# DeltaNet attention and an MLP in one kernel: VectorE's constants and GpSimd's row selector moved to the beginning, W1's first half asked for later

## The chip, the cores and the metric

The kernel runs on one core of a Trainium2 chip. The metric is the time of one launch in device microseconds (us), the median of several runs. The core has five engines that run their own instruction streams and meet at semaphores: TensorE (PE; its weight loads are listed as PEld), VectorE (DVE), ScalarE (ACT), GpSimd (POOL) and SyncE (SP, which here only issues DMA). Sixteen DMA engines move data between HBM and the on-chip memory SBUF; matmuls write PSUM, eight banks of accumulators.

## The reference

```python
B, H, S, D = 4, 8, 768, 48
k_n = k / (np.linalg.norm(k, axis=-1, keepdims=True) + 1e-06)
state = np.zeros((B, H, D, D))
for t in range(S):
    kt, vt, bt = k_n[:, :, t], v[:, :, t], beta[:, :, t, None]
    y[:, :, t] = np.einsum('bhd,bhde->bhe', q[:, :, t], state)
    v_old = np.einsum('bhde,bhd->bhe', state, kt)
    state = state + bt[:, :, :, None] * np.einsum('bhd,bhe->bhde', kt, vt - v_old)
x = y.transpose(0, 2, 1, 3).reshape(B * S, H * D)      # 3072 x 384
h = x @ w_in                                            # 384 x 2048
g = 0.5 * h * (1.0 + np.tanh(c * (h + 0.044715 * h * h * h)))   # c = sqrt(2/pi)
return g @ w_out                                        # 3072 x 384
```

A recurrent delta rule over 768 steps for 32 heads, then an MLP on its output.

## The kernel before

The 768 steps are cut into 12 chunks of 64 (c = 0 to 11). A chunk has two units, u = 2c and 2c + 1, of 8 heads for two batches each. Per chunk the recurrence becomes matrix work: the keys are normed and turned, their products (a lower triangle) are inverted, the state is carried from chunk to chunk, and the chunk's 256 rows go through the MLP, 16 `up` and 8 `down` groups of matmuls.

The steps carry names, and the name's number is the unit or the chunk. Those that follow come up below, roughly in the order of the data:

- `k2.01`, `q1.11`, `v0.00`, `k0x0.01`: loads of a chunk's k, q, v in four pieces (line 472). Chunk 0's k comes in two halves, `k0x1` and `k0x0`. Three buffers per input, so chunk c + 3 overwrites chunk c.
- `sq`, `sum`, `pow`, `eps`, `inv` (lines 495 to 503): the norms of the keys, on ScalarE, VectorE and, for `eps` sometimes, GpSimd. `0a` and `0b` are the halves of chunk 0.
- `kn` or `knc` (lines 531, 524): keys times inverse norm; `qb`, `qbc`, `vb`, `vbc`: casts of q and v to bf16.
- `Tk`, `Tq`, `T` (line 540): transposes on TensorE, copied back by `kTk`, `kTq`, `kT` (line 343); `GD`, `GQ`, `G` (line 564): products of keys with keys and queries, read by `dn` (copy) and `wq` (masked copy, line 571).
- `F`, `lp`, `x0`, `L`, `xm`, `xa`, `xb` (lines 633 to 669): the inverses of the 8x8 blocks, `xm1` to `xa6` step by step on VectorE. `F` uses the constant `sel`, `L` the constant `rows`.
- `xe`, `xec`, `KZ`, `kz`, `GM`, `lw`, `X10`, `X11`, `A4`, `rt4`, `B4`, `bde4`, and so on (lines 599 to 723): the inverse of the whole triangle.
- `V`, `R`, `U`, `Un`, `S`, `Sn`, `O`, `On`, `X`, `xT` (lines 756 to 811): state and output of a chunk; `up`, `gelu`, `down`, `Z` (lines 824 to 840): the MLP.
- `betaT`, `betaN`, `betaH`, `betaL`, `betaS`, `betaC` (lines 437 to 460): beta is turned and spread once.
- Constants, made once: `sel` (line 391), `unit` (394), `rowz` and `rows1` (381, 382: `rows` is zeroed, then GpSimd sets its ones), `two` (380), `wz` (355), `muq` (369), `low1` (396), `first0` (400, a column of a leaf buffer), `triwq` and `trilw` (411 on GpSimd, 343 elsewhere: patterns in the buffers of `wq` and `lw`), `ladj` (418, patterns in a right-hand side), `pad` (403) and `bdz` (421, zeroes).

Nothing is scheduled at run time. The text `ORDER` lists every step once with its engine (`:d` VectorE, `:g` GpSimd, `:a` ScalarE, `:s` SP, none for TensorE) and its PSUM bank (`@4`). `Flow.order` (line 151) fills one queue per engine from it, and `Flow.emit` (line 190) puts semaphore waits where an operand comes from another engine. An engine runs its queue strictly in the order of the text, so a step that waits holds everything behind it on its engine. Of two GpSimd steps for different halves of the partitions, the later waits for the earlier.

The weights are loaded by GpSimd's DMA queue, in two halves each. W1's halves (`w1.0`, `w1.1`) are declared as readers of chunk 1's k buffer, so that they come after its load:

```python
A(("pool",), f"w1.{i}", lambda e, P, f0=f0: e.dma_start(W1[:, :, f0:f0 + FF // 2], w1v[:, :, f0:f0 + FF // 2]),
  reads=["kraw10", "kraw11"], writes=[f"W1{i}"], dma=f"w1{i}")
```

Chunk 4's k goes to the same buffer, and so its four loads wait for both halves of W1. They stand in SP's queue behind all earlier loads.

Of the kernel before, what the change touches and what calls it, by code (L numbers as in the profile page):

```python
# [21 lines left out]
muq1:g ladj4.0:a k2.01:s betaN011:d pow.1:a betaN110:d eps.1:g pad3:d k2.11:s inv.1:d triwq1:d betaN010:d low1:d kn.2:d v0.10:s kn.3:d qb.1:a Tk.2@7
v0.01:s qb.0:g Tk.3@5 kTk.2:d q2.01:s rows1:g Tq.1@4 sq.0a:a betaN111:d kTk.1:d q2.10:s kTq.1:d kTk.3:a sum.0a:d q2.00:s GD.3@4 betaH1:d pow.0a:a
Tq.0@7 sq.2:a eps.0a:d rpad0:g v1.00:s inv.0a:d GD.2@2 betaN000:d GD.1@0 dn.3:a kn.0:g betaL1:d q1.01:s betaH0:d betaS1@6 dn.2:a sum.2:d low2:g
q1.00:s dn.1:a Tk.0@4 first0:d F.1@2 kTq.0:d pow.2:a q1.10:s eps.2:g kTk.0:d trilw2:g q1.11:s GQ.1@0 lp.1:d GD.0@4 betaL0:d x0.1:d L.1@7 q3.01:s
dn.0:a two:d inv.2:d GQ.0@2 wz:d knc.2:g xm1.1:d qbc.2:a F.0@4 k3.00:s wq.0:d xa1.1:d q3.10:s betaS0@5 xm2.1:d xa2.1:d betaS3@2 w1.0:g lp.0:d k3.11:s
betaC0:a xm3.1:d ladj5.1:d L.0@3 triwq2:a ladj4.1:d T.5@4 v0.00:s x0.0:d wqa.1:a xm1.0:d first1:g xa1.0:d kT.5:a qb.3:g xa3.1:d xm2.0:d v0.11:s
xa2.0:d trilw3:g Tq.3@0 xm4.1:d xm3.0:d betaC1:a xa3.0:d qb.2:g xa4.1:d xm5.1:d xm4.0:d T.4@6 xa4.0:d xa5.1:d betaS2@1 xm5.0:d xm6.1:d kT.4:a xa6.1:d
xa5.0:d Tq.2@4 kTq.3:d xb.1:g xm6.0:d triwq5:g xa6.0:d betaC2:a xb.0:d G.5@6 w1.1:g kTq.2:a xe.1:d G.4@0 dn.4:a v2.11:s xe.0:d KZ.1@4 kz.1:a wq.4:d
mwp1:g dn.5:a GM.1@4 xec.1:d KZ.0@0 ladj5.0:a F.2@3 wqa.5:a betaC3:a lw.1:d kz.0:a lp.2:d bdz1:d L.2@3 k3.01:s GM.0@4 x0.2:d X10.1:g KZ.2@6 lw.0:d  # L30
KZ.3@0 kz.3:a X11.1:g kz.2:a xm1.2:d GM.3@0 xa1.2:d rpad1:g A4.1@2 X11.0:g lw.3:d X10.0:g rt4.1:d k3.10:s xm2.2:d A4.0@1 X11.3:g xa2.2:d v1.01:s
B4.1@2 xm3.2:d xa3.2:d rt4.0:d q3.11:s GQ.2@6 GM.2@4 vb.0:a xm4.2:d vb.1:g wq.2:d k4.11:s B4.0@1 bde40.1:a triwq3:g lw.2:d V.0@6 X10.3:g k4.01:s
bde41.1:a bde40.0:a k4.00:s wqb.1:g xa4.2:d A4.3@2 xm5.2:d bde41.0:a A5.1@0 k4.10:s rt4.3:d GQ.3@4 R.0:a rt5.1:d A5.0@1 X11.2:g B4.3@2 v1.10:s rt5.0:d
B5.1@0 bde40.3:a xa5.2:d q3.00:s B5.0@7 X10.2:g xm6.2:d fill115@1 xa6.2:d be50.1:d be50.0:a v1.11:s wq.3:d xb.2:g be51.1:a A4.2@3 sq.3:a w2.0:g
be51.0:d v2.01:s xe.4:d U.0@0 bde41.3:d KZ.4@4 Un.0:a w2.1:g rt4.2:d kz.4:a O.0@6 sum.3:d A5.3@4 On.0:a S.0@2 rt5.3:d GM.4@0 sq.4:a xe.5:d X.0@6
B4.2@7 lw.4:d Sn.0:a fill85@4 KZ.5@4 xT.0:a sum.4:d X11.4:g bde40.2:a up4.0@2 kz.5:d pow.3:g up0.0@0 bde41.2:a up1.0 X10.4:d tabG:a up2.0 up12.0@6
qbc.3:d up3.0 A5.2@4 up13.0 rt5.2:d gelu0.0:a up5.0 up6.0 GM.5@4 eps.3:d inv.3:d knc.3:d up7.0 up14.0 A4.4@0 lw.5:d up15.0 turn.7:s B5.2@1 gelu3.0:a
rt4.4:d up8.0@4 X11.5:g up9.0 gelu1.0:a B5.3@0 vbc.1:g down00.0@6 be50.3:d up10.0 be51.3:a X10.5:d pow.4:g be50.2:a up11.0 V.1@2 gelu2.0:a T.6@0
v2.00:s A4.5@7 kT.6:d v2.10:s be51.2:a K.1 down01.0 R.1:a rt4.5:d q5.00:s G.6@4 k5.10:s B4.5@7 dn.6:a B4.4@2 xi4.5:d U.1@0 bde40.4:a down02.0 k5.00:s
wq.6:d bdc40.5:g Un.1:a down03.0 k5.01:s bde41.4:d bdc41.5:g eps.4:g A5.5@1 k5.11:s Z0.0:d wqb.5:g S.1@4 Q.1@2 q4.11:s Sn.1:d G.7@6 O.1 vbc.2:g  # L40
q4.01:s A5.4@0 rt5.5:d On.1:a down10.0@5 inv.4:d q4.10:s dn.7:d kn.9:g down11.0 rt5.4:d q4.00:s wq.7:d F.3@1 q5.01:s B5.4@4 lp.3:d V.2@2 sq.5:a x0.3:d
v3.10:s L.3@1 B5.5@0 xm1.3:d X.1@6 be50.4:a v3.01:s be50.5:a xa1.3:d K.2 be51.5:a xm2.3:d down12.0 be51.4:a xa2.3:d q5.11:s xT.1:d R.2:a down13.0
xm3.3:d q5.10:s xa3.3:d xm4.3:d qbc.4:g up0.1@2 xa4.3:d Z1.0:a up12.1@6 xm5.3:d xa5.3:d up1.1 kn.8:g xm6.3:d sum.5:d turn.9:s U.2@4 up13.1 Un.2:a
up14.1 xa6.3:d pow.5:g xb.3:d up15.1 xec.3:d Q.2@0 gelu3.1:a S.2@4 turn.8:s O.2 up2.1 Sn.2:d On.2:a up3.1 up8.1@6 gelu0.1:a qb.11:d up9.1 KZ.6@0
eps.5:d KZ.7@4 inv.5:d kz.6:a up10.1 kn.11:d up11.1 kz.7:a up4.1@0 kn.10:g turn.11:s qb.10:a GM.6@2 gelu2.1:a G.9@4 lw.6:d up5.1 up6.1 dn.9:a up7.1
# [858 lines left out]
```

## Time and profile before

| what | value |
|---|---|
| median of 3 runs | 254.64 us (254.40 to 255.61) |
| span of the profiled execution (no other time is given for it) | 254.7 us |
| PE busy over the span | 226.0 us (89%) |
| DVE busy over the span | 185.8 us (73%) |
| ACT busy over the span | 157.4 us (62%) |
| POOL busy over the span | 130.1 us (51%) |
| mean granted TensorE clock | 0.966 |

The profile is one execution. Its page has the busy time of each engine, the span in 40 slices of 6.4 us (a digit is the busy share in tenths; PEclk is the granted clock of TensorE in tenths of full speed), the DMA queues, the chain of waits that ended last, and groups of equal instructions:

```profile
PE   0259558899999998999999899999999999999994
DVE  6599989955996989898888779898494665755100
POOL 7647448347563397627358968472535525330000
PEclk9999956689999999999999999999999999999999
```

The first eight slices are the start that the change touches. Beside the page the trace can be asked for a stretch: the time line gives start and length in us, engine, line, operation, what it writes and reads, how many were merged, and in brackets the idle time of the engine ahead of it and what ended it. The waits of SP's queue are a view of their own:

```profile
SPq L472 <- DMA W<-in_moe_w_in_dram: 5.9, 1, 5.9
```

That is one wait of 5.9 us, of the k loads of chunk 4 for W1.

### The profile page before, as it was taken

The numbers are of one execution on the slowest core, as the hardware profiler recorded it, in microseconds if no ns is written. First come the engines' busy times: TensorE is split into PE (matmuls) and PEld (weight loads), VectorE is DVE, ScalarE is ACT, GpSimd is POOL, SyncE is SP. The second block draws the span as 40 slices with busy tenths as digits, with TensorE's granted clock in tenths as the row PEclk, the third lists the DMA queues.
The fourth block names the chain that finished last, engine by engine and source line by source line (L and its number), as shares of the span: only waits on it lengthen the run. The fifth ranks groups of instructions, "written<-read, shape, count | busy, mean of one in ns | idle before, by whom it ended". The sixth has DMA issues, their size and how long they took to land.

```text
span 254.7 us, 12256 instructions
## 1 busy us (share of the span) xinstructions
PE 226.0 (89%) x5500; PEld 178.3 (70%) x5502; DVE 185.8 (73%) x445; ACT 157.4 (62%) x244; POOL 130.1 (51%) x159
## 2 busy tenths in 40 slices
PE   0259558899999998999999899999999999999994
...
DVE  6599989955996989898888779898494665755100
...
POOL 7647448347563397627358968472535525330000
PEclk9999956689999999999999999999999999999999
...
GB/s 103 165 144 118 184 162 95 165 127 117 128 130 105 112 126 124 135 165 147 119 146 167 100 36 131 147 153 130 56 93 167 62 49 4 33 68 64 3 93 62
DMA packets 104532, 28.25 MB, mean 111 GB/s; under 512 B 98592, under 2 KB 103712, under 8 KB 104480
## 3 DMA queue, kind: packets, MB, share of 16 engines
q1 hardware_dynamic: 99200, 23.79, 54.0%
...
q8 instruction: 43, 0.70, 1.2%
q10 hardware_dynamic: 2400, 0.54, 1.1%
...
HBM read 20.64 MB, written 4.72 MB: 100 GB/s over the span
## 4 chain that ended last, share of the span: by engine, by line
PE 73%; DVE 15%; ACT 4%; DMA 2%; ACTq 2%; issue 2%; SPq 1%; POOL 0%
PE ps L835 24%; PE ps L824 22%; PE ps L692 5%; PE ps L620 3%; PE ps L752 3%; PE ps L773 2%; DMA vraw<-in_v_dram 2%; PE ps L697 2%; PE ps L564 2%; DVE lw L623 2%; DVE xl L658 2%; PE ps L633 2%; PE ps L759 2%; DVE ps L655 2%; PE ps L609 1%
## 5 line engine op out<-in xcount | busy, mean ns | idle before, releaser
L824 PE MATMUL ps<-xT,W 128*128 128x256 bf16 x576 | 76.8, 277 | 0.4 <-DVE xl L658 0.4
L835 PE MATMUL ps<-W,gT 128*128 128x384 bf16 x384 | 72.7, 326 | 0.0
L828 ACT ACTIVATE gT<-ps 128x1024 bf16<-128x1024 f32 x48 | 48.4, 1022 | 26.4 <-PE ps L824 25.8
L824 PEld LDWEIGHTS ps<-xT,W 128*128 128x128 bf16 x576 | 52.2, 99 | 9.3 <-DVE xl L658 0.5
L835 PEld LDWEIGHTS ps<-W,gT 128*128 128x128 bf16 x384 | 34.0, 97 | 18.2
L682 POOL TENSOR_SCALAR_AFFINE_SELECT bd<-lw 64x512 bf16<-64x512 bf16 x34 | 22.6, 667 | 37.7 <-DVE lw L623 28.6
L704 DVE TENSOR_TENSOR rl<-ps,two 128x384 bf16<-128x384 f32 (+1 forms) x48 | 22.9, 484 | 9.7 <-PE ps L692 9.5
L623 DVE CAST_PREDICATED lw<-mlw,ps 128x832 bf16<-128x832 uint16 x24 | 24.3, 1018 | 6.8 <-PE ps L620 6.5
L499 POOL TENSOR_TENSOR nrm<-nrm,half 128x16 f32<-128x16 f32 x9 | 26.6, 2956 | 2.8 <-DVE nrm L497 2.7
L343 ACT ACTIVATE bd<-ps 32x256 bf16<-32x256 f32 (+1 forms) x40 | 16.8, 428 | 8.2 <-PE ps L692 4.4
L692 PEld LDWEIGHTS ps<-lw,bd 128*128 128x128 bf16 x384 | 15.5, 98 | 4.2 <-POOL bd L682 1.2
L692 PE MATMUL ps<-lw,bd 128*128 128x32 bf16 (+1 forms) x384 | 17.2, 183 | 1.2 <-POOL bd L682 1.1
L658 DVE TENSOR_TENSOR xl<-ps,xl 128x96 bf16<-128x96 f32 (+4 forms) x72 | 16.0, 228 | 2.0
L655 DVE TENSOR_TENSOR ps<-ps,xl 128x64 f32<-128x64 f32 (+5 forms) x72 | 15.6, 221 | 2.0 <-PE ps L649 0.5
L343 ACT ACTIVATE ob<-ps 128x384 f32<-128x384 f32 x17 | 8.3, 490 | 14.0 <-PE ps L835 14.0
L722 POOL COPY bd<-xi 64x256 f32<-64x256 f32 x20 | 8.0, 401 | 16.4 <-ACT xi L343 8.5
L540 PE MATMUL ps<-ident,tok 128*128 128x128 bf16 x80 | 7.8, 246 | 8.1 <-POOL tok L531 3.8
L531 POOL TENSOR_TENSOR tok<-kraw,nrm 128x384 bf16<-128x384 f32 x9 | 8.5, 945 | 12.7 <-DVE bsb L349 5.6
L349 ACT ACTIVATE kT<-ps 128x512 bf16<-128x512 f32 x18 | 10.4, 596 | 6.4 <-PE ps L609 6.4
L343 ACT ACTIVATE dn<-ps 128x512 bf16<-128x512 f32 x18 | 10.4, 593 | 5.3 <-PE ps L564 5.3
L620 PE MATMUL ps<-kT 48*64 48x56 bf16 (+1 forms) x768 | 11.1, 196 | 2.8 <-ACT kT L349 1.4
L599 POOL TENSOR_TENSOR zt<-xb,blk 128x2048 bf16<-128x2048 bf16 x3 | 10.9, 3642 | 4.1 <-DVE xb L669 3.9
...
## 6 DMA issues: line engine op xcount, KB each, us to landing
qraw<-in_q_dram SPq DMA_DIRECT2D x48, 96.0 KB, 3.6
vraw<-in_v_dram SPq DMA_DIRECT2D x48, 96.0 KB, 3.5
kraw<-in_k_dram SPq DMA_DIRECT2D x44, 96.0 KB, 3.6
...
out_dram<-ob SPq DMA_DIRECT2D x3, 96.0 KB, 2.2
```

The costliest lines, as they stand in the source:

```text
L343: return e.activation(out, in_, ACT.Copy) if e is nc.scalar else e.tensor_copy(out, in_)
L499: if e is nc.scalar else e.tensor_tensor(nr[:, 1, hx], nr[:, 0, hx], half[:, hx], ALU.pow), reads=[nrn, "half"] + ["one"] * (c < ROOTS),
L620: ins = e.matmul(P(ps("GM"))[hf(a), o_ + c0:o_ + c1], kT[s][r, y, g, hf(a)], kT[s][r, z, g, C * a + c0:C * a + c1])
L623: A(("dve",), op("lw"), lambda e, P: e.copy_predicated(lw[m][:, :, 0:LW - LB], mlw[:, :, :].rearrange("p w t -> p (w t)")[:, 16:16 + LW - ...
L655: A(("dve",), f"xm{m}.{c}", lambda e, P, m=m, w=w, part=part: e.tensor_tensor(part(P), P(f"L.{c}")[:, off[m]:off[m] + 2 * H * w].rearrange ...
L658: A(("dve",), f"xa{m}.{c}", lambda e, P, m=m, part=part: e.tensor_tensor(xl[y][:, :, m + 1:LB], part(P), xl[y][:, :, m + 1:LB], ALU.add), ...
L682: A(("pool", "dve"), op(f"X1{a}"), lambda e, P, src=lw[m][hf(a), :, LW - C:LW], dst=bd[b_][hf(a), :, hf(a)], a=a: e.affine_select(out=dst, ...
L692: ins = e.matmul(P(name)[:, C * h + c0:C * h + c1], bd[b_][:, h, :], rhs[:, h, :])
L704: A(("dve",), op(f"rt{i}"), lambda e, P, i=i, c0=c0, c1=c1, r_=r_: e.tensor_tensor(r_[:, 0:H, c0:c1], P(ps(f"A{i}")).rearrange("p (h t) -> ...
L824: ins = e.matmul(P(ph)[:, 256 * f:256 * f + 256].rearrange("p (x t) -> p x t", x=2), W1[:, j, 128 * (i + f):128 * (i + f) + 128], x_[:, :, ...
L828: A(("act",), f"gelu{i // 4}.{c}", lambda e, P, i=i, ph=ph: e.activation(g_[:, i:i + 4, :], P(ph).rearrange("p (f t) -> p f t", f=4), ACT. ...
L835: ins = e.matmul(P(po)[:, 0:DM], g_[:, f, 128 * b:128 * b + 128], W2[:, f, :], start=(f == 0), stop=(f == FC - 1))
```

## The change

Only the text `ORDER` differs; every step is the same and stays on its engine. On VectorE, `two`, `wz`, `ladj5.1` and `ladj4.1` go ahead of `sel`; `first0` behind `unit`; `bdz1` behind `muq`; `triwq1`, `pad3` and `low1` ahead of `sum.0b`; and `inv.1`, `kn.2`, `kn.3` ahead of three of the `betaN` copies. On GpSimd, `rowz` and `rows1` go behind `triwq0`, `triwq4` behind `qb.0`, and `w1.0` behind `qb.3`, `trilw3` and `qb.2`, the casts of chunk 1's queries. Of the text, one line of before and the two that stand in its place:

```diff
-ident2:g bdz0:g k0x1.01:s k0x1.11:a mmlw:d identf:d blk2:g k1.00:s beta00:a blk3:g k0x0.00:a k1.10:s half:g own:g triwq4:g trilw1:a k1.11:s sel:d
+ident2:g bdz0:g k0x1.01:s k0x1.11:a mmlw:d identf:d blk2:g k1.00:s beta00:a blk3:g k0x0.00:a k1.10:s half:g own:g trilw1:a k1.11:s two:d wz:d
+ladj5.1:d ladj4.1:d sel:d q0.10:s k0x0.10:a unit:d first0:d betaT1@0 triwq0:g rowz:g rows1:g q0.01:s mmuq:d bdz1:d mln0:g tabS:a bdz2:g sq.0b:a
```

How the queues change is shown at three places, rows with their line, operation and tile; a minus is a row of before that is gone from there, a plus one that is there now. First the beginning of VectorE's queue, from the memset of the mask `mlw` to the first beta copy (`sel` is line 391, `unit` 394, `muq` 369):

```order
 L368 MEMSET mlw 128x128
 L364 TENSOR_SCALAR identf<-tmpl 32x32
+L380 TENSOR_SCALAR two<-tmpl 128x64
+L355 MEMSET wz 128x256
+L418 TENSOR_SCALAR rl_1<-tmpl 128x8x32
+L418 TENSOR_SCALAR rl_1<-tmpl 128x8x16
 L391 TENSOR_TENSOR sel<-ident,own 128x1024
 L394 TENSOR_REDUCE unit<-ident 128x8
+L400 CAST xl<-unit 128x16
 L369 MEMSET muq 128x64
+L421 MEMSET bd 128x512
 L349 TENSOR_SCALAR bsb<-ps 64x22x4
```

`two`, `wz` and both `ladj` now stand ahead of `sel`, `first0` behind `unit`, `bdz1` behind `muq`. GpSimd's queue at the same time, from the memset of `half` and the sum `own` on, which `sel` reads:

```order
 L367 MEMSET half 128x16
 L390 TENSOR_TENSOR own<-blk 128x64
-L411 COPY wq<-tmpl 128x256 x2
+L411 COPY wq<-tmpl 128x256
+L381 MEMSET rows 128x512
+L382 AFFINE_SELECT rows<-rows 128x1024
 L372 AFFINE_SELECT mlw<-mlw 64x64
 L421 MEMSET bd 128x512
 L403 MEMSET tok 128x16x8
 L374 AFFINE_SELECT mlw<-mlw 64x64
-L381 MEMSET rows 128x512
```

One of two pattern copies has left, and the row selector (line 382) has come with its memset, 10 rows earlier than before. Second place, VectorE from `sum.1` (line 497) to the first `kT` copy of chunk 1 (line 343); line 503 is `inv.1`, line 531 are `kn.2` and `kn.3`, line 349 the `betaN` copies:

```order
 L497 TENSOR_REDUCE nrm<-sq 128x16
+L503 RECIPROCAL nrm<-nrm 128x16
+L531 TENSOR_TENSOR tok<-kraw,nrm 128x8x48 x2
 L349 TENSOR_SCALAR bsb<-ps 64x2x4
 L349 TENSOR_SCALAR bsb<-ps 64x22x4
-L403 MEMSET tok 128x16x8
-L503 RECIPROCAL nrm<-nrm 128x16
-L343 COPY wq<-tmpl 128x512
 L349 TENSOR_SCALAR bsb<-ps 64x2x4
-L396 MEMSET low 128x1
-L531 TENSOR_TENSOR tok<-kraw,nrm 128x8x48 x2
 L343 COPY kT<-ps 128x512
```

The two products follow `inv.1` at once; the pad, the pattern and the memset have gone to the beginning. Third place, GpSimd from the pattern copy `trilw2` and chunk 2's key product `knc.2` (line 524) to `xb.1` (line 669):

```order
 L411 COPY lw<-tmpl 128x448
 L524 TENSOR_TENSOR tok<-kraw,nrm 128x2x8x48
-L481 DMA W<-in_moe_w_in_dram 128x3x1024
 L400 CAST xl<-unit 128x16
 L343 CAST tok<-qraw 128x8x48
 L411 COPY lw<-tmpl 128x448
 L343 CAST tok<-qraw 128x8x48
+L481 DMA W<-in_moe_w_in_dram 128x3x1024
 L669 TENSOR_TENSOR xb<-xl,bc 128x128
 L411 COPY wq<-tmpl 128x256
```

The request for W1's first half has passed four steps. The one for the second half stays where it was, behind `xb.1` and a pattern copy. VectorE in the same stretch, from `lp.0` (line 637) on, in the queue before:

```order
L637 TENSOR_TENSOR lp<-ps,bsb 128x112
L655 TENSOR_TENSOR ps<-ps,xl 128x64
L418 TENSOR_SCALAR rl_1<-tmpl 128x8x32
L418 TENSOR_SCALAR rl_1<-tmpl 128x8x16
L640 SCALAR_TENSOR_TENSOR xl<-lp,unit 128x16x7
L655 TENSOR_TENSOR ps<-ps,xl 128x96
```

and in the queue of the change:

```order
L637 TENSOR_TENSOR lp<-ps,bsb 128x112
L655 TENSOR_TENSOR ps<-ps,xl 128x64
L640 SCALAR_TENSOR_TENSOR xl<-lp,unit 128x16x7
L655 TENSOR_TENSOR ps<-ps,xl 128x96
L658 TENSOR_TENSOR xl<-ps,xl 128x16x6
```

The two `ladj` (line 418) no longer stand ahead of `x0.0` (line 640) and `xm1.0`. TensorE, ScalarE and SP keep their queues as they were.

More of the change, by code (lines that the diff above doesn't have):

```diff
@@ L22 @@
[L22 to L45, printed above, removed]
@@ new lines @@
+k2.00:s pad4:g mwp0:g betaN101:d triwq1:d pad3:d low1:d k0x0.11:a betaT0@6 sum.0b:d q0.00:s betaN100:d mln1:g pow.0b:a q0.11:s eps.0b:d pad1:g
+inv.0b:d betaN001:d sq.1:a kn.1:g q2.11:s k0x0.01:a sum.1:d k2.10:s muq0:g Tk.1@1 muq1:g ladj4.0:a k2.01:s pow.1:a eps.1:g k2.11:s inv.1:d kn.2:d
+v0.10:s kn.3:d qb.1:a Tk.2@7 v0.01:s qb.0:g triwq4:g Tk.3@5 betaN011:d betaN110:d betaN010:d kTk.2:d q2.01:s Tq.1@4 sq.0a:a betaN111:d kTk.1:d q2.10:s
+kTq.1:d kTk.3:a sum.0a:d q2.00:s GD.3@4 betaH1:d pow.0a:a Tq.0@7 sq.2:a eps.0a:d rpad0:g v1.00:s inv.0a:d GD.2@2 betaN000:d GD.1@0 dn.3:a kn.0:g
```

27 lines of the change are left out of this document (23 added, 4 removed).

## The prediction

> **What bounds the kernel now.** I read the busy times by stage first, then the chain of waits up to the first MLP matmul, and then the time lines of VectorE and GpSimd beside each other. In the two stage rows the columns behind the stage's length are busy microseconds (and instructions) of PE, PEld, DVE, ACT and POOL, then the granted TensorE clock.
>
> ```profile
> span 254.7 us, 12256 instructions
> 22.00:34.00 12.00, 6.93 (x212) 5.60 (x203) 11.53 (x39) 8.96 (x17) 5.97 (x10) 0.95 0.96 155
> 50.00:100.00 50.00, 49.09 (x1294) 38.79 (x1293) 40.18 (x98) 37.56 (x60) 29.94 (x28) 0.97 0.79 123
> ```
>
> From 50 us on TensorE is busy 49 of each 50 us, in an order that the change leaves alone: this part can start earlier or later, hardly run shorter. Before it, from 22 to 34 us, VectorE is busy 11.53 of 12 us and TensorE only 6.93. So a start of 50 us that VectorE bounds is followed by a rest that TensorE bounds. The chain of waits over the first 51 us says the same (start, length, what):
>
> ```profile
> 12.39 0.43 DVE wq L343
> 13.06 1.97 DVE tok L531
> 20.21 0.11 DVE xl L400
> 50.01 1.18 PE ps L824 x5
> ```
>
> It runs mostly over VectorE until the first `up` (line 824) at 50.01, and pieces of it are constants that nobody needs yet: `triwq1` at 12.39, `first0` at 20.21. So a microsecond taken out of this stretch should start the MLP a microsecond earlier.
>
> **Part A, 11.5 to 15.7 us.**
>
> ```profile
> 12.17 0.50 POOL L343 CAST tok<-qraw 128x384 bf16<-128x384 f32 x1
> 12.31 0.51 DVE L343 COPY wq<-tmpl 128x512 bf16<-128x512 bf16 x1
> 12.63 2.05 POOL L382 TENSOR_SCALAR_AFFINE_SELECT rows<-rows 128x1024 bf16<-128x1024 bf16 x1
> 13.06 1.96 DVE L531 TENSOR_TENSOR tok<-kraw,nrm 128x384 bf16<-128x384 f32 x1
> 14.95 0.54 DVE L531 TENSOR_TENSOR tok<-kraw,nrm 128x384 bf16<-128x384 f32 x1
> 15.72 0.42 DVE L343 COPY kT<-ps 128x512 bf16<-128x512 bf16 x1 [0.23 <-PE ps L540]
> ```
>
> `kn.2` (13.06) and `kn.3` (14.95) are the same instruction, yet the first takes 1.96 us and the second 0.54. The first ends 0.3 us after GpSimd's row selector `rows1` (12.63 + 2.05 = 14.68): it stood still for about 1.4 us beside the selector. The change takes the selector away from there, and `pad3`, `triwq1` and `low1` from in front of `kn.2`; three beta copies move behind `kn.3`. `inv.1` keeps its place, since it waits for GpSimd, and ends at 12.39, where the chain goes on with `triwq1`. Then `kn.2` runs from 12.39 to 12.9 at best. GpSimd's query cast (until 12.67) and the `triwq4` behind it may hold the two products in the same way, so `kn.2` ends at 13.2 at worst, and `kn.3` between 13.4 and 13.9 instead of 15.49. The three beta copies come next (about 0.5 together), and the first `kT` copy starts between 13.9 and 14.4 instead of 15.72. That is 1.3 to 1.8 us; I take **1.5**. What is late next is chunk 0's last k load, for which `sq.0a` waits:
>
> ```profile
> 13.85 0.52 ACT L495 ACTIVATE sq<-kraw 128x384 f32<-128x384 f32 x1 [1.19 <-DMA kraw<-in_k_dram]
> ```
>
> It is done at 14.37; its reader `sum.0a` stands on VectorE behind three `kT` copies, which would end near 15.7. The load stays hidden.
>
> **Part B, 20 to 22.3 us.** `first0`, `two` and `wz` leave.
>
> ```profile
> 20.14 0.18 DVE L400 CAST xl<-unit 128x16 bf16<-128x16 f32 x1
> 21.77 0.43 PE L564 MATMUL ps<-kT 48*64 48x64 bf16 x16
> 22.29 0.67 DVE L571 CAST_PREDICATED wq<-muq,ps 128x512 bf16<-128x512 uint16 x1
> ```
>
> `first0` holds 0.11 of the chain, so **0.1**. `two` and `wz` I put at 0: the masked copy at 22.29 reads what the matmuls leave at 22.20, and those do not wait for the two. The upper end is the 0.35 that they hold on VectorE.
>
> **Part C, 23.9 to 25.4 us.**
>
> ```profile
> 23.45 1.01 POOL L481 DMA_DIRECT2D W<-in_moe_w_in_dram  x1
> 23.79 0.22 DVE L655 TENSOR_TENSOR ps<-ps,xl 128x64 f32<-128x64 f32 x1
> 23.92 0.94 DVE L418 TENSOR_SCALAR rl<-tmpl 128x256 bf16<-128x256 bf16 x2
> 24.62 0.59 POOL L343 CAST tok<-qraw 128x384 bf16<-128x384 f32 x1
> 24.78 0.56 DVE L640 SCALAR_TENSOR_TENSOR xl<-lp,unit 128x112 bf16<-128x112 bf16 x1
> 25.38 0.27 DVE L655 TENSOR_TENSOR ps<-ps,xl 128x96 f32<-128x96 f32 x1
> 34.12 0.20 DVE L640 SCALAR_TENSOR_TENSOR xl<-lp,unit 128x112 bf16<-128x112 bf16 x1
> ```
>
> The two `ladj` copies take 0.94 us beside the issue of W1's first half on GpSimd, and `x0.0` takes 0.56 beside a GpSimd cast, against 0.20 for the same shape at 34.12. Without the copies `x0.0` starts at 24.01 and `xm1.0` at 24.3 to 24.4 instead of 25.38: 1.0 us. If a query cast, which W1 no longer holds back, lies beside `x0.0` again, 0.6 is left. I take **0.9**, since the cast would mostly be over. W1's issue now falls among the `xm` and `xa`, which take one operand from PSUM; the `xm` at 23.79, beside the issue, and at 25.38, beside other GpSimd work, show 0.22 and 0.27 for 64 and 96 elements, so it costs them nothing.
>
> **Part D, nothing.** `bdz1` (0.48 us, now at 33.7) stands ahead of `lw.0`, which waits for TensorE in any case:
>
> ```profile
> 34.79 1.02 DVE L623 CAST_PREDICATED lw<-mlw,ps 128x832 bf16<-128x832 uint16 x1 [0.46 <-PE ps L620]
> ```
>
> If TensorE were not in the way, `bdz1` could give 0.4; I put it at 0. W1's first half is needed at 50 us and asked for at about 23.5, as before: 0.
>
> **Where the moved work goes.**
>
> ```profile
> 4.62 1.38 DVE L391 TENSOR_TENSOR sel<-ident,own 128x1024 bf16<-128x1024 bf16 x1 [1.22 <-POOL own L390]
> 7.35 0.24 DVE L349 TENSOR_SCALAR bsb<-ps 64x88 f32<-64x88 f32 x1 [0.98 <-PE ps L437]
> 9.00 0.55 DVE L497 TENSOR_REDUCE nrm<-sq 128x8 f32<-128x384 f32 x1 [1.40 <-ACT sq L495]
> 10.32 0.83 POOL L531 TENSOR_TENSOR tok<-kraw,nrm 128x384 bf16<-128x384 f32 x1 [1.86 <-DVE bsb L349]
> ```
>
> VectorE idles 1.22 us before `sel` (for `two`, `wz` and the `ladj`: 1.38 at their present lengths, less if they no longer stand beside a DMA issue), 0.98 before 7.35 (for `first0` and `bdz1`: 0.66) and 1.40 before 9.00 (for `triwq1`, `pad3`, `low1`: 0.74). GpSimd idles 1.86 us before 10.32; the selector (2.05) comes in there and `triwq4` (0.4) goes out. By length all fit, and what is 0.2 over before `sel` finds 0.3 before 7.35. Cost 0.
>
> **The sum:** 1.5 + 0.1 + 0.9 = 2.5 us. Against the profiled execution (span 254.7; the page shows no time around it, and the median of the runs, 254.64, lies within 0.1) that is **252.2 us**. The lower ends give 1.3 + 0.1 + 0.6 = 2.0 (252.7), the upper ones 1.8 + 0.45 + 1.0 + 0.4 = 3.6 (251.1).
>
> **Rival 1: the stall moves with the selector.** In its new place the selector starts when `sel` ends, near 6.0, and runs to 8.0, and `first0` lies beside it. A cast of this shape has stood still beside GpSimd work:
>
> ```profile
> 18.45 0.88 POOL L531 TENSOR_TENSOR tok<-kraw,nrm 128x384 bf16<-128x384 f32 x1 [3.69 <-DVE bsb L349]
> 18.56 0.80 DVE L447 CAST bhl<-bsb 128x16 bf16<-128x16 f32 x1
> ```
>
> That is 0.80 against the 0.18 of `first0` at 20.14. All that is queued behind `first0` on VectorE (`muq`, `bdz1`, a beta copy, `triwq1`, `pad3`, `low1`: about 1.6 us) would start at 8.0, and `sum.0b` at 9.6 instead of 9.00; for it wait, over ScalarE, chunk 0's last k load, `sq.1`, `sum.1` and `inv.1`. GpSimd's query cast would have cost `kn.2` up to 0.3 of these 0.6 anyway, so I price it at 0.3 to 0.6, 0.5 taken: **252.7**. [...]
>
> **Rival 2: loads that keep their absolute time.** Behind the landings below stands the median time from issue; q0 is GpSimd's queue from 26 to 30 us.
>
> ```profile
> 29.16 0.81 POOL L481 DMA_DIRECT2D W<-in_moe_w_in_dram  x1
> q0 software_dynamic: 326, 0.67, 92.9%
> vraw<-in_v_dram SPq DMA_DIRECT2D x1, 96.0 KB, 8.8
> 38.96 0.59 ACT L343 ACTIVATE bd<-ps 64x512 bf16<-64x512 f32 x1 [2.24 <-PE ps L692]
> 38.11 3.40 SPq L472 DMA_DIRECT2D kraw<-in_k_dram  x4
> kraw<-in_k_dram SPq DMA_DIRECT2D x4, 96.0 KB, 3.4
> 43.78 1.81 POOL L483 DMA_DIRECT2D W<-in_moe_w_out_dram  x2
> 47.38 0.84 ACT L495 ACTIVATE sq<-kraw 128x768 f32<-128x768 f32 x1
> ```
>
> While W1 moves, it takes 92.9% of the DMA engines, and a load issued behind it needs 8.8 us. Its second half, behind `xb.1`, would be asked for at 26.7 instead of 29.16, so that both halves run without a gap to 35 or 38 us, and chunk 0's v may have to wait for their end. On ScalarE `vb.0`, now done at 36.7 (2.24 us before 38.96), may end at 36.5 without harm, so v may land by 36.0. At 38 the gain is down to 0.5: **254.2**.
>
> **Rival 3, slower.** Chunk 4's k loads wait for W1's second half, at 38.11, since W1 is declared to read their buffer; the fourth is issued 2.8 us later and lands after 3.4, at 44.3. `sq.4`, on ScalarE ahead of the copies that feed the first `up`, would be due at 44.9, and W2's issue at 41.3 instead of 43.78. If W1 lands at 39 or later (all transfers at once), the fourth k load goes out at 41.8, behind W2, and needs some 8.8 us, like a load behind W1: it lands at 50.6, `sq.4` starts 3.2 us later than before, **257.9**. It decides from a landing of W1 at about 38.5 on. Against it: W1 is asked for earlier, and outruns the other loads.
>
> **Rival 4: the earlier start is not passed on.**
>
> ```profile
> 50.00:53.40 3.40, 3.40 (x19) 2.42 (x18) 1.55 (x4) 2.17 (x4) 2.97 (x2) 0.50 1.31 204
> ```
>
> TensorE runs the first `up` at a clock of 0.50. If the full clock came no earlier than now, 2.5 us more would run at half speed, and half the gain were gone; with most of rival 1 on top, 0.7 is left: **254.0**.
>
> **How the numbers follow.** Forecast 0.50, rival 1 0.20, rival 2 0.10, rival 3 0.08, rival 4 0.12. About 0.5% (1.3 us) is what a measurement of this kernel can tell from no change. The forecast and rival 1 are faster by more: 0.70. Rivals 2 and 4 lie within it: 0.22. Rival 3 is slower: 0.08. The range goes from the upper ends, 251.1, to rival 2, 254.3; rival 3 and the outermost edges are left out.
>
> **What would show it.** `kn.2` at 0.55 us, over by 13.2; the first `kT` copy near 14.2; `xm1.0` near 22.8; the first `up` near 47.5, and TensorE as busy as before behind it. Rival 1: `first0` of a microsecond or more, `sum.0b` at 9.5. Rival 2: `vb.0` after 36. Rival 3: `sq.4` after 47.4. I am wrong if the first `up` comes 2.5 us earlier and the end does not follow, or if VectorE still stands still in the first 15 us.

## The result, and the profile after

| | before | with the change |
|---|---|---|
| median of 6 runs each, on one chip | 254.33 us (253.46 to 255.61) | 251.87 us (251.61 to 252.48) |
| ratio, 95% interval | | 0.990 (0.9866 to 0.9934) |
| span of the profiled execution | 254.7 us | 250.0 us |
| its own time | not given | 251.9 us |
| mean granted clock | 0.966 | 0.973 |

The change makes the kernel 2.46 us faster (the interval is 1.7 to 3.4 us); 252.2 had been forecast. A second measurement of the same two kernels, among the experiments, gave 254.34 and 252.27: 2.07 us, ratio 0.9922 (0.9889 to 0.9955). Ratios and intervals are formed from fast executions alone, so a ratio need not equal the quotient of the two medians.

The two spans differ by more, 4.7 us. But 1.9 us of the profiled run of after lie around its span (251.9 less 250.0), and in its other runs 1.8 to 1.9. The 254.7 us of before are therefore, by estimate, a run of about 256.6 us, longer than any of the six timed ones. The first experiment looks into that.

The page of after, for the span as a whole, with the rows that were shown of before:

```profile
span 250.0 us, 12255 instructions
PE   0268568899989998999999999999999999999994
DVE  6898989967968989898789878997493775654100
POOL 7837268457462597546368988454436617220000
PEclk9999956799999999999999999999999999999999
```

VectorE is busier in the second slice, from about 6 to 12.5 us (8 where it had 5): the constants have come into its idle time. What the steps of the prediction look like now is in the time lines. First VectorE from the first beta copy on (`sum.0b` 9.22, `kn.2` and `kn.3` 12.63, three beta copies 13.99, the first `kT` copy 14.44), and with it the constant `sel`, GpSimd's selector and `triwq4` (columns: start, length, engine, line, operation, what it writes and reads):

```profile
4.90 1.38 DVE L391 TENSOR_TENSOR sel<-ident,own 128x1024 bf16<-128x1024 bf16 x1 [0.83 <-POOL own L390]
5.82 2.33 POOL L382 TENSOR_SCALAR_AFFINE_SELECT rows<-rows 128x1024 bf16<-128x1024 bf16 x1 [0.15 <-POOL rows L381]
6.61 1.59 DVE L400 CAST xl<-unit 128x16 bf16<-128x16 f32 x1
9.22 0.54 DVE L497 TENSOR_REDUCE nrm<-sq 128x8 f32<-128x384 f32 x1
12.63 1.32 DVE L531 TENSOR_TENSOR tok<-kraw,nrm 128x384 bf16<-128x384 f32 x2
12.82 0.72 POOL L411 COPY wq<-tmpl 128x256 f32<-128x256 f32 x1
13.99 0.42 DVE L349 TENSOR_SCALAR bsb<-ps 64x8 f32<-64x8 f32 x3
14.44 0.42 DVE L343 COPY kT<-ps 128x512 bf16<-128x512 bf16 x1
```

`kn.2` and `kn.3` take 1.32 us together instead of 2.43 (13.06 to 15.49), and the first `kT` copy starts 1.28 us earlier. The selector has not become harmless: `first0`, 0.18 us long at its old place, now lies beside it and takes 1.59. That is rival 1, though `sum.0b` comes only 0.22 us later, not 0.6.

VectorE around `x0.0` (line 640) and `xm1.0` (line 655, 23.48), ahead of them the masked copy `wq.0`, and the matmuls `L.0` (line 649), whose result `xm1.0` reads:

```profile
20.94 0.69 DVE L571 CAST_PREDICATED wq<-muq,ps 128x512 bf16<-128x512 uint16 x1
22.27 0.27 DVE L637 TENSOR_TENSOR lp<-ps,bsb 128x112 bf16<-128x112 f32 x1
22.45 0.22 DVE L655 TENSOR_TENSOR ps<-ps,xl 128x64 f32<-128x64 f32 x1
22.58 0.33 DVE L640 SCALAR_TENSOR_TENSOR xl<-lp,unit 128x112 bf16<-128x112 bf16 x1
22.59 0.38 PE L649 MATMUL ps<-lp,rows 128*128 128x96 bf16 x6
23.48 0.27 DVE L655 TENSOR_TENSOR ps<-ps,xl 128x96 f32<-128x96 f32 x1 [0.56 <-PE ps L540]
```

`x0.0` starts 2.20 us earlier than before (24.78), `xm1.0` only 1.90 (25.38): between the two there are now 0.56 us in which VectorE does nothing. Before, `xm1.0` followed at once.

And the places that the rivals named: `lw.0` on VectorE, `vb.0` and `sq.4` on ScalarE, the first `up` on TensorE; and, in a fence of its own, the stage that TensorE bounds (columns as in the prediction):

```profile
32.82 1.02 DVE L623 CAST_PREDICATED lw<-mlw,ps 128x832 bf16<-128x832 uint16 x1 [0.30 <-PE ps L620]
34.23 0.52 ACT L343 ACTIVATE vb<-vraw 128x384 bf16<-128x384 f32 x1
45.41 0.83 ACT L495 ACTIVATE sq<-kraw 128x768 f32<-128x768 f32 x1
47.70 2.79 PE L824 MATMUL ps<-xT,W 128*128 128x256 bf16 x18
```

```profile
50.00:100.00 50.00, 48.30 (x1381) 38.83 (x1378) 41.10 (x97) 37.76 (x59) 30.73 (x30) 1.00 0.82 127
```

`vb.0` and `sq.4` come 2 us earlier with everything else and wait for no load (no idle time is noted before them), so rivals 2 and 3 did not happen. The first `up` is at 47.70 instead of 49.94 (so the time line; the chain of before has its piece at 50.01), and behind it TensorE is as busy as before.

### The profile page after: what moved, and what is told of

It reads as the page before. It is cut to its first block, busy times and chain, and to the rows that moved or that the text cites. A ratio compares the mean times of both kernels' runs of the same rounds, so it can differ in the third digit from the quotient of the medians.

```text
span 250.0 us, 12255 instructions
## 1 busy us (share of the span) xinstructions
PE 224.4 (90%) x5500; PEld 177.2 (71%) x5502; DVE 185.5 (74%) x445; ACT 157.0 (63%) x244; POOL 130.0 (52%) x159
## 4 chain that ended last, share of the span: by engine, by line
PE 77%; DVE 15%; POOL 2%; ACT 2%; issue 2%; ACTq 0%; POOLq 0%
PE ps L835 26%; PE ps L824 22%; PE ps L692 5%; PE ps L620 3%; PE ps L752 3%; PE ps L564 3%; PE ps L633 2%; PE ps L773 2%; PE ps L697 2%; DVE xl L658 2%; PE ps L759 2%; PE ps L795 2%; DVE lw L623 2%; DVE ps L655 1%; PE ps L540 1%
## 5 line engine op out<-in xcount | busy, mean ns | idle before, releaser
L824 PE MATMUL ps<-xT,W 128*128 128x256 bf16 x576 | 75.7, 274 | 0.0
L824 PEld LDWEIGHTS ps<-xT,W 128*128 128x128 bf16 x576 | 51.6, 98 | 8.5 <-ACT kT L349 0.2
```

Source lines behind the costliest of these rows:

```text
L824: ins = e.matmul(P(ph)[:, 256 * f:256 * f + 256].rearrange("p (x t) -> p x t", x=2), W1[:, j, 128 * (i + f):128 * (i + f) + 128], x_[:, :, ...
```

## The experiments

Theory 1 is the prediction's, as far as the traces bear it out: the selector no longer stalls `kn.2`, `ladj` is out of the way, the start is some 2 us shorter, and the end follows. The rivals are that the constants carry the gain, that W1's move does, or that the end does not follow the start. The table has what was measured; "first kT" is the first `kT` copy of chunk 1. Kernels of one group ran on one chip and share the runs of before (medians 254.21, 254.35 and 254.34 us).

| run | first kT | xm1.0 | first up | span | median | ratio (95%) |
|---|---|---|---|---|---|---|
| before, first profile | 15.72 | 25.38 | 49.94 | 254.7 | | |
| the change, first profile | 14.44 | 23.48 | 47.70 | 250.0 | 251.87 | 0.990 (0.9866 to 0.9934) |
| e1_before_again | 15.57 | 25.24 | 49.80 | 251.5 | 253.24 (one run) | |
| e2_selector | 14.04 | 23.71 | 49.62 | 252.4 | 252.85 | 0.9956 (0.9922 to 0.9990) |
| e3_vector | 15.77 | 24.56 | 49.07 | 252.2 | 253.58 | 0.9972 (0.9943 to 1.0001) |
| e4_w1 | 15.57 | 25.08 | 49.63 | 251.6 | 253.84 | 0.9971 (0.9937 to 1.0005) |
| e5_w1_back | 14.46 | 23.27 | 49.95 | 251.8 | 252.83 | 0.9935 (0.9906 to 0.9963) |
| e6_ladj_back | 14.40 | 24.04 | 48.62 | 251.9 | 252.40 | 0.9924 (0.9893 to 0.9954) |
| e7_first0 | 14.24 | 23.02 | 47.58 | 249.4 | 251.27 | 0.9875 (0.9841 to 0.9908) |
| e8_t5_later | 14.23 | 23.21 | 48.29 | 252.5 | 254.23 (one run) | |
| e9_after_again | 14.44 | 23.23 | 47.53 | 250.0 | 252.27 | 0.9922 (0.9889 to 0.9955) |
| e10_w1_back_again | 14.48 | 23.33 | 47.98 | 251.1 | 252.76 | 0.9937 (0.9906 to 0.9968) |
| e11_no_stalls | 13.79 | 22.59 | 47.16 | 249.1 | 251.53 | 0.9886 (0.9845 to 0.9928) |
| e12_no_stalls_w1_back | 13.79 | 22.75 | 47.82 | 251.1 | 252.44 | 0.9918 (0.9879 to 0.9957) |

### Before, profiled again (e1_before_again, no edit)

> The kernel before, unchanged, profiled a second time. Of its first profile the span (254.7 us) is as long as the median of its runs, while in the kernel with the change 1.9 us of each run lie outside the span (251.9 against 250.0). Theory 1: the first profile caught a long execution, and the 4.7 us by which the spans differ are about 2 us of change and 2 to 3 us of differences between executions. Then this profile has a span of 252 to 253 us and a run about 1.9 us above it; up to the first up the rows stand where they stood within 0.2 us (kn.2 1.9 to 2.0 us, first kT copy at 15.7, first up at 49.9 to 50.0), and what is gone is gone behind the first up. Rival: the span of before is 254.7 whenever it is profiled, and the change gains over 4 us inside the span: then this span is 254.4 to 255.

The span is 251.5 us, 3.2 us shorter, while the first `up` stands only 0.14 us earlier. The selector and the two products, and behind them the busy time of two stretches, the one that VectorE bounds and the one in which the first `up`s run:

```profile
12.78 0.55 DVE L531 TENSOR_TENSOR tok<-kraw,nrm 128x384 bf16<-128x384 f32 x1
12.86 2.34 POOL L382 TENSOR_SCALAR_AFFINE_SELECT rows<-rows 128x1024 bf16<-128x1024 bf16 x1
13.25 2.28 DVE L531 TENSOR_TENSOR tok<-kraw,nrm 128x384 bf16<-128x384 f32 x1
```

```profile
22.00:34.00 12.00, 7.73 (x208) 6.34 (x200) 11.53 (x40) 8.82 (x16) 5.87 (x10) 0.82 0.96 162
50.10:53.40 3.30, 3.30 (x51) 2.77 (x53) 2.13 (x6) 2.96 (x4) 2.83 (x1) 0.98 1.31 204
```

Two things are to be seen. First, this time it is `kn.3` that stands still, not `kn.2`: `kn.2` had begun just ahead of the selector (12.78 against 12.86) and took 0.55, and `kn.3` ended at 15.53, 0.33 after the selector. The expectation that `kn.2` takes 1.9 to 2.0 again was wrong in the instruction, right in the sum; the product that stands still ends 0.33 to 0.34 us after the selector, whichever of the two it is (here `kn.3`, in the first profile `kn.2`, at 15.02 for 14.68). Second, TensorE got through 51 matmuls from 50.10 to 53.40 at a clock of 0.98, where the first profile has 19 from 50.00 to 53.40 at 0.50. So, by estimate, about half of the 3.2 us is a clock that in the first profile came back 3.3 us later (half of 3.3 is 1.65), and it belongs to the execution, since the kernel is the same. The mean clock over the span is 0.966 in both profiles: the second has more of its half clock between 22 and 34 us (0.82 there, against 0.95), where VectorE is busy for 11.53 us either way, so that it costs little. A further piece of the 3.2 us is a gap of TensorE that the first profile has on its chain of waits, in front of line 620, and the second has not; the profile shows nothing that it waits for ("issue"):

```profile
140.51 0.73 issue
```

Theory 1 holds in the main: most of the 4.7 us belongs to the execution. The span fell even below the 252 to 253 us that were expected; 1.5 us are left between it and the span of the change, and this execution (253.24) is itself 1 us faster than the median of before (254.21). What the change is worth is read from the medians.

### Its parts alone (e2_selector, e3_vector, e4_w1)

GpSimd's part alone, from before:

```diff
-k1.10:s half:g own:g triwq4:g trilw1:a k1.11:s sel:d
+k1.10:s half:g own:g trilw1:a k1.11:s sel:d
...
-unit:d betaT1@0 triwq0:g q0.01:s mmuq:d
+unit:d betaT1@0 triwq0:g rowz:g rows1:g q0.01:s mmuq:d
...
-betaT0@6 sum.0b:d rowz:g q0.00:s
+betaT0@6 sum.0b:d q0.00:s
...
-v0.01:s qb.0:g Tk.3@5 kTk.2:d q2.01:s rows1:g Tq.1@4
+v0.01:s qb.0:g triwq4:g Tk.3@5 kTk.2:d q2.01:s Tq.1@4
```

> Only GpSimd's part at the beginning: rowz and rows1 behind triwq0, triwq4 behind qb.0; VectorE's queue and W1 as before. Theory 1 (the gain is the stall of kn.2 beside the selector, and ladj): kn.2 falls from 1.96 to 0.55 to 0.8 us, sum.0b stays at 9.0 since first0 does not lie beside the selector here, the first kT copy comes 1.0 to 1.3 us earlier (14.4 to 14.7), and the time is 1.0 to 1.3 us below before (253.0 to 253.3 where before has 254.3). Rival 2 (the constants that leave VectorE's chain are what counts, since the selector only stalls something else): kn.2 is short, but the gain at the first kT copy is below 0.4 us and the time within 0.4 of before. Rival 3 (W1 and the clock): no gain at the end.

The two products, and the first `kT` copy behind them:

```profile
12.78 0.56 DVE L531 TENSOR_TENSOR tok<-kraw,nrm 128x384 bf16<-128x384 f32 x1
13.25 0.75 DVE L531 TENSOR_TENSOR tok<-kraw,nrm 128x384 bf16<-128x384 f32 x1
14.04 0.43 DVE L343 COPY kT<-ps 128x512 bf16<-128x512 bf16 x1
```

The first `kT` copy comes 1.53 us earlier than in the second profile of before, more than the 1.0 to 1.3 that were expected and more than in the whole change (1.13). The selector alone gives all that the change gains at this place: rival 2, by which the stall only moves and the constants count, falls. The time is 1.36 us below before in the medians, by the ratio 0.25 to 2.0 us. At the first `up` of this profile only 0.18 us of the 1.53 are left, mainly because of one gap of TensorE in front of line 620 that waits for nothing that the profile shows:

```profile
47.09 0.63 PE L620 MATMUL ps<-kT 48*64 48x56 bf16 x32 [1.15 <-issue]
```

Such gaps come up again below. The converse, the change with the selector, `rowz` and `triwq4` in their old places:

```diff
-betaT1@0 triwq0:g rowz:g rows1:g q0.01:s mmuq:d
+betaT1@0 triwq0:g q0.01:s mmuq:d
...
-half:g own:g trilw1:a k1.11:s
+half:g own:g triwq4:g trilw1:a k1.11:s
...
-k2.00:s pad4:g mwp0:g betaN101:d
+k2.00:s pad4:g mwp0:g rowz:g betaN101:d
...
-v0.01:s qb.0:g triwq4:g Tk.3@5 betaN011:d
+v0.01:s qb.0:g rows1:g Tk.3@5 betaN011:d
```

> The change with the selector put back: rowz, rows1 and triwq4 in their places of before, all of VectorE's moves and W1's as in the change. Theory 1: inv.1 ends near 12.2, kn.2 or kn.3 now stands still beside rows1 until about 14.7, so that the first kT copy gains only 0.4 to 0.8 us of the change's 1.3 (14.9 to 15.3); ladj still gives 0.6 at xm1.0; the time is 0.9 to 1.4 us below before, against 2.46 for the change. Rival 2: the constants alone bring over 1.8 us. Rival 3 (W1): as much as the change.

VectorE from `kn.2` to the first `kT` copy, in this kernel, and the selector:

```profile
12.63 2.32 POOL L382 TENSOR_SCALAR_AFFINE_SELECT rows<-rows 128x1024 bf16<-128x1024 bf16 x1
12.43 0.66 DVE L531 TENSOR_TENSOR tok<-kraw,nrm 128x384 bf16<-128x384 f32 x1
13.01 2.28 DVE L531 TENSOR_TENSOR tok<-kraw,nrm 128x384 bf16<-128x384 f32 x1
15.32 0.42 DVE L349 TENSOR_SCALAR bsb<-ps 64x8 f32<-64x8 f32 x3
15.77 0.42 DVE L343 COPY kT<-ps 128x512 bf16<-128x512 bf16 x1
```

With the constants out of the way `kn.2` starts 0.35 us earlier (12.43 against 12.78), but `kn.3` still waits for the selector's end (12.63 and 2.32 long, so 14.95), and then the beta copies follow. The first `kT` copy gains nothing; 0.4 to 0.8 us had been expected, so theory 1 had still put too much on the constants. The 0.68 us that `xm1.0` gains over the second profile of before come behind that place, where `ladj` is gone, and the time is 0.63 us below before (interval 0 to 1.4; 0.9 to 1.4 had been expected).

W1's request alone, from before:

```diff
-xm2.1:d xa2.1:d betaS3@2 w1.0:g lp.0:d k3.11:s
+xm2.1:d xa2.1:d betaS3@2 lp.0:d k3.11:s
...
-xa3.0:d qb.2:g xa4.1:d xm5.1:d
+xa3.0:d qb.2:g w1.0:g xa4.1:d xm5.1:d
```

> Only the request for W1's first half moved, behind qb.2; all constants and the selector as before. Theory 1: the two ladj no longer lie beside the issue but beside a GpSimd cast, xm1.0 moves by at most 0.3 us, W1 lands within 1 us of before, the time is the same within 0.4 us. Rival 3 (the loads are what the change gains by): at least 1 us faster. If ladj's 0.94 us was all a stall beside the issue of W1, xm1.0 comes 0.3 to 0.5 us earlier and the time falls by as much.

`xm1.0` comes 0.16 us earlier than in the second profile of before; the two `ladj` take 0.73 us there, beside the casts. The median is 0.37 us below before, an interval from 1.6 us faster to 0.1 slower. At the start the parts nearly add up: the 1.53 of e2 and the 0.68 of e3, which holds W1's move too, are 2.2 at `xm1.0`, where the change has 1.76 to 2.01. In the medians 1.36 (e2) and 0.63 (e3) are 1.99, where the change has 2.07 to 2.46.

### Parts put back, and a stall removed (e5 to e8)

The change with W1's request back ahead of the query casts:

```diff
-qb.2:g w1.0:g xa4.1:d xm5.1:d
+qb.2:g xa4.1:d xm5.1:d
...
-GQ.0@2 knc.2:g xm1.1:d qbc.2:a
+GQ.0@2 knc.2:g w1.0:g xm1.1:d qbc.2:a
```

> The change with only W1's request put back ahead of first1 and qb.3. Theory 1: the issue (1.0 us on GpSimd) now stands from about 22.1 to 23.1 and pushes the two query casts back by 1 us; x0.0 lies beside the issue, not beside a cast, and stays at 0.2 to 0.35 us; xm1.0 stays within 0.3 us of 23.48, the first up within 0.4 us of 47.7, and the time within 0.6 us of the change. Rival 3 (the W1 move carries the gain): the first up comes 1 us or more later than 47.7 and the time is within 1.2 us of before.

The start is that of the change (`xm1.0` 23.27, `x0.0` 0.33 us), as theory 1 has it. The rest of the expectation failed: the first `up` is 2.25 us later than in the change's first profile (0.4 had been allowed), and the median is 0.96 us above the change's, which was measured on another chip (0.6 had been allowed). TensorE's gaps hold most of the 2.25: 1.20 us in front of line 620, and 0.93, 0.56 and 0.36 in front of lines 633, 692 and 609.

```profile
47.42 0.63 PE L620 MATMUL ps<-kT 48*64 48x56 bf16 x32 [1.20 <-issue]
```

The change with only the two `ladj` back:

```diff
-k1.11:s two:d wz:d ladj5.1:d ladj4.1:d sel:d
+k1.11:s two:d wz:d sel:d
...
-betaC0:a xm3.1:d L.0@3
+betaC0:a xm3.1:d ladj5.1:d ladj4.1:d L.0@3
```

> The change with only the two ladj put back between xm3.1 and x0.0. Theory 1: they take 0.5 to 0.95 us there beside the casts, x0.0 ends 0.5 to 0.9 us later, and since xm1.0 had 0.56 us of idle time in front of it in the change, it comes 0.2 to 0.7 us later (23.7 to 24.2); the first up moves by the same, and the time is 0.2 to 0.7 us above the change. Rival 4 (the end does not follow the start): xm1.0 moves, the first up or the end does not.

VectorE at that place:

```profile
22.55 0.93 DVE L418 TENSOR_SCALAR rl<-tmpl 128x256 bf16<-128x256 bf16 x2
23.39 0.61 DVE L640 SCALAR_TENSOR_TENSOR xl<-lp,unit 128x112 bf16<-128x112 bf16 x1
24.04 0.27 DVE L655 TENSOR_TENSOR ps<-ps,xl 128x96 f32<-128x96 f32 x1
```

The copies take 0.93 us beside the casts, about as long as they did beside W1's issue (0.94), `x0.0` takes 0.61 again, and `xm1.0` is 0.56 us later than in the change's first profile (0.81 later than in its second). The idle time in front of `xm1.0` is gone. The first `up` is 0.9 to 1.1 us later. The time, 252.40, does not tell it from the change.

The change with `first0` where the selector is over:

```diff
-unit:d first0:d betaT1@0
+unit:d betaT1@0
...
-pad3:d low1:d k0x0.11:a
+pad3:d low1:d first0:d k0x0.11:a
```

> The change with first0 behind low1, when the selector is over. Theory 1: first0 takes 0.2 us instead of 1.59, sum.0b stands at 9.0 again (9.22 in the change), inv.1, the first kT copy and xm1.0 come 0.2 us earlier, which no timing resolves. Rival 1 in its strong form (the stall costs 0.5 us or more): the first kT copy comes 0.5 us or more earlier than 14.44. If another instruction stands still beside the selector in first0's place (bdz1, triwq1), sum.0b stays at 9.2.

`first0` and `sum.0b` there:

```profile
8.37 0.73 DVE L400 CAST xl<-unit 128x16 bf16<-128x16 f32 x1
8.99 0.55 DVE L497 TENSOR_REDUCE nrm<-sq 128x8 f32<-128x384 f32 x1
```

`first0` still takes 0.73 instead of 0.18, now beside small GpSimd work, but no longer pushes anything: `sum.0b` is back at 8.99, and the first `kT` copy is 0.20 us earlier. So rival 1 cost the change 0.2 us, not the 0.5 that it was priced at. Even these 0.2 are not in every execution: in the profile of e8 (below), which leaves `first0` beside the selector, the selector begins 0.26 us earlier (5.56), `first0` stands still as long (1.60), and `sum.0b` is at 9.00.

Last, the question of the 0.56 us in front of `xm1.0`, which the profile puts down to the transposes of line 540. They go behind the next group on TensorE:

```diff
-xm3.1:d L.0@3 triwq2:a T.5@4 v0.00:s x0.0:d
+xm3.1:d L.0@3 triwq2:a v0.00:s x0.0:d
...
-first1:g xa1.0:d kT.5:a qb.3:g
+first1:g xa1.0:d qb.3:g
...
-trilw3:g Tq.3@0 xm4.1:d
+trilw3:g Tq.3@0 T.5@4 kT.5:a xm4.1:d
```

> The change with the transposes T.5 and their copy kT.5 behind Tq.3. In the change xm1.0 (23.48) starts 0.57 us after its operand x0.0 is done and 0.5 us after L.0 is done, but 0.06 us after T.5's first transposes end, which it does not read. If it is held by TensorE's transposes, it now starts within 0.1 us of the end of L.0 or x0.0, near 23.0 to 23.1. If it is held by something else (the GpSimd copy trilw3, that ends at 23.33, or the fetch of instructions), it stays at 23.4 to 23.5. The copy kT.5 comes about 1 us later here, so that later rows may lose what this gives.

TensorE with `L.0` and the first transposes, VectorE with `x0.0` and `xm1.0`:

```profile
22.31 0.38 PE L649 MATMUL ps<-lp,rows 128*128 128x96 bf16 x6 [0.20 <-DVE lp L637]
23.09 0.83 PE L540 MATMUL ps<-ident,tok 128*128 128x128 bf16 x12 [0.40 <-ACT wq L343]
22.30 0.57 DVE L640 SCALAR_TENSOR_TENSOR xl<-lp,unit 128x112 bf16<-128x112 bf16 x1
23.21 0.27 DVE L655 TENSOR_TENSOR ps<-ps,xl 128x96 f32<-128x96 f32 x1 [0.34 <-DVE xl L640]
```

The transposes begin only at 23.09, 0.12 us before `xm1.0`, and end far behind its start, so they cannot have released it. `L.0` was done at 22.69 (22.31 and 0.38), `x0.0` at 22.87. The transposes fall as the cause: `xm1.0` starts 0.52 us after the end of `L.0` here, and 0.51 in the change's first profile (22.97 to 23.48). The same 0.51 or 0.52 stand in all nine profiles in which `x0.0` is over in time (the change, e3, e5 and e7 to e12), while the distance from the end of `x0.0` goes from 0.31 (e7) to 0.58 (e10). So `xm1.0` there follows `L.0`, not `x0.0`. Before, it started 0.04 us after `x0.0` (25.34), and `L.0` had been done for a microsecond (24.30):

```profile
23.92 0.38 PE L649 MATMUL ps<-lp,rows 128*128 128x96 bf16 x6
```

What VectorE does in that half microsecond stays open.

### The change again, W1 again, and a version without the stalls (e9 to e12)

> The change, unchanged, timed and profiled again beside the next three. Theory 1: up to 30 us its rows stand where they stood in its first profile within 0.25 us (first kT copy 14.2 to 14.5, xm1.0 23.2 to 23.5, again 0.45 us behind the wait in front of it); behind that, gaps of TensorE that wait for nothing (issue) come at other places or in other sizes and move the end by up to 1.5 us. Ratio to before 0.987 to 0.993.

No edit. The first `kT` copy stands at 14.44 again, `xm1.0` at 23.23, the ratio within what was expected. The first `up`s, which in the first profile began at half clock, run at full clock here:

```profile
47.53:50.93 3.40, 3.40 (x51) 2.91 (x55) 2.22 (x5) 3.28 (x5) 3.30 (x2) 1.00 1.29 190
```

The kernel of e5 once more, beside it:

> W1's request put back, as in e5_w1_back, now on the same chip as the change. Before with only W1 moved came out 0.3% below before, and the change with only W1 put back 0.35% above what the change had against its own before: each alone is within its interval. Theory 1: W1's place is worth nothing, the median is within 0.5 us of e9_after_again, and the gap of 1.2 us in front of the key products at 46.2 us is absent or elsewhere. Rival 3: it is worth 0.6 to 0.9 us, the median is that much above e9_after_again, and the gap stands at 46 us again.

The gap of 1.2 us in front of line 620 is absent in the same kernel, so W1's place alone does not make it. The median is 0.49 us above the change's, at the edge of the 0.5 that theory 1 allows. The first `up` is 0.45 us later than in e9, but it also meets another clock. The granted clock of the change (e9) stands first here, that of e10 second; the eighth slice runs from about 44 to 50 us:

```profile
PEclk9999957999999999999999999999999999999998
PEclk9999957599999999999999999999999999999999
```

Then the change with three edits, each against a wait of VectorE:

```diff
-unit:d first0:d betaT1@0
+unit:d betaT1@0
...
-pad3:d low1:d k0x0.11:a
+pad3:d low1:d first0:d k0x0.11:a
...
-eps.1:g k2.11:s inv.1:d kn.2:d
+eps.1:g k2.11:s betaN011:d betaN110:d betaN010:d inv.1:d kn.2:d
...
-qb.0:g triwq4:g Tk.3@5 betaN011:d betaN110:d betaN010:d kTk.2:d
+qb.0:g Tk.3@5 kTk.2:d
...
-sum.2:d low2:g q1.00:s
+sum.2:d low2:g triwq4:g q1.00:s
```

> The change with first0 behind low1 (as in e7_first0), the three beta copies betaN011, betaN110, betaN010 back in front of inv.1, where VectorE idles 0.63 us, and triwq4 on GpSimd behind low2 instead of beside kn.3. Theory 1: the beta copies cost 0.42 us between kn.3 and the first kT copy, the stall of kn.3 0.2, that of first0 0.2: inv.1 stays at 12.13, kn.3 0.55, the first kT copy at 13.6 to 13.7 (14.44 in the change), xm1.0 22.3 to 22.6, the first up near 47.0, and the time 0.5 to 0.9 us below the change. Rival: another wait takes their place (chunk 0's last k load for sq.0a, or the query transposes), the first kT copy comes earlier but xm1.0 gains less than 0.3 us.

The two products and the first `kT` copy:

```profile
12.43 1.13 DVE L531 TENSOR_TENSOR tok<-kraw,nrm 128x384 bf16<-128x384 f32 x2
13.79 0.42 DVE L343 COPY kT<-ps 128x512 bf16<-128x512 bf16 x1 [0.23 <-PE ps L540]
```

The first `kT` copy is 0.65 us earlier than in the change and now waits 0.23 us for its transposes: VectorE is no longer the limit there. `xm1.0` gains 0.64 to 0.89, the first `up` 0.37 to 0.54, the median 0.74. That is the fastest start of all; but its interval and the change's overlap, so that the time alone does not show it to be faster. e7, with one of the three edits, has a median as low (251.27).

And the same with W1's request put back as in e5:

> e11_no_stalls with W1's request back ahead of first1 and qb.3: a second pair for the question of W1. Theory 1: within 0.5 us of e11_no_stalls. Rival 3: 0.6 to 0.9 us above it.

The median is 0.91 us above e11_no_stalls. The four comparisons on W1 (e4 against before, e5 and e10 against the change, e12 against e11) all point the same way, by 0.4 to 1.0 us, and none by more than the intervals leave open. At `xm1.0` the four pairs differ by 0.2 us at most; at the first `up` they differ by 0.17, 2.25, 0.45 and 0.66, the same way again. But e5 has its gaps there, and e10 and e12 run TensorE at a clock of 0.50 from 44 to 50 us, where e9 and e11 have 1.00 (the six matmuls of line 807 take 0.82 us in e10 and e12 and 0.51 in e9 and e11); so the later `up` cannot be laid to W1's place by these profiles. Whether W1's place is worth half a microsecond stays open.

## Why the prediction was right, step by step

**The bound: right.** Between the first profiles of the two kernels the start became shorter by 1.90 us at `xm1.0` and by 2.24 at the first `up`, between their second ones by 2.01 and 2.27. The medians fell by 2.46 and 2.07. TensorE behind it is busy for 48.3 of 50 us.

**The time that the sum was made against: wrong, without harm.** The text held that the span of 254.7 us and the median of 254.64 are the same execution time to 0.1. They are not: 1.7 to 1.9 us lie around the span in the timed runs, and that execution was some 2 us longer than the median. The two errors cancel, and the sum was in effect taken from the median.

**The sum, 2.5: the trace has 1.9 to 2.0 of it at `xm1.0`.** That is the lower end of what the text added up (2.0). That 252.2 lies between the two measured medians (251.87 and 252.27) is in part luck: the gain was put high, and the time that it was taken from lay 0.4 us above the medians of before that were measured later (254.33 and 254.34). The text's range ends at 254.3, though rival 2, which it names for that end, is worked out as 254.2; nothing hangs on it.

**Part A, 1.5 us: the mechanism right, 1.1 to 1.3 measured.** The selector alone gives 1.53 (e2), and without it VectorE's constants give nothing (e3). They count only once the selector is gone: in e11 `kn.2` starts 0.35 us earlier than in e2 (12.43 for 12.78) and the first `kT` copy 0.25 (13.79 for 14.04), with `first0` and `triwq4` out of the way too. The forecast for the first `kT` copy, 13.9 to 14.4, was missed by 0.04 at its end, since `inv.1` came 0.2 us late and the two products took another 0.2 beside `triwq4` (1.32 together, 1.13 in e11). The three beta copies behind `kn.3` cost 0.45 (13.99 to 14.44; about 0.5 was expected), and e11 shows that they need not.

**Moved work at no cost: wrong by 0.2 us.** It fitted by its length, but `first0` stood still beside the selector, as rival 1 had it, which pushed `sum.0b` by 0.22; e7 gives these 0.2 back. Rival 1's price (0.5) was too high: of the 1.4 us that `first0` stood still, VectorE's idle time up to `sum.0b` took up 1.2. By its own sign ("if VectorE still stands still in the first 15 us") the text was wrong at this place.

**Part B, 0.1: 0.1 and 0.3 measured.** `wq.0` is at 20.94 instead of 22.29, 1.35 us earlier, of which 1.28 are part A; in the second profiles it is 1.46 earlier (20.70 for 22.16), of which 1.13 are part A. Both lie within the text's upper end.

**Part C, 0.9: 0.55 to 0.8 measured.** `ladj` does give its 0.9 at `x0.0` (22.58 for 24.78: 2.20, less 1.35 for parts A and B, is 0.85; the second profiles give 0.85 too). At `xm1.0` 0.55 is left in both pairs (1.90 less 1.35, 2.01 less 1.46). The step that failed is that `xm1.0` would start behind `x0.0`: it starts 0.51 us behind the end of `L.0`, a wait that the text did not have. e6 puts 0.56 to 0.81 us back at `xm1.0`; in the time its median (252.40) does not show them.

**Part D, 0: as forecast.** `lw.0` still waits for TensorE (0.30 us) in the change.

**W1, 0: not settled;** the four comparisons give 0.4 to 1.0 us, and their intervals do not exclude 0. **Rival 4** fell: the end follows the start. The half clock at the first `up`s was measured again, but its length differs between executions of one kernel: 3.4, 0.3, 1.4 and 0 us in four profiles of two kernels (before, before; the change, the change). The full clock, which the rival had come no earlier than in before (53.40), was there from 49.10 in the change's first profile.
